# Cached attention with an MLP beside it, on one core: all large loads in one in-order stream through a ring of slots, a softmax per group of four key heads, scores in four column tiles, output weights last

## The chip, the cores and the metric

The kernel runs on one core of a Trainium2 chip. Times are device microseconds (us) of the whole program, medians of several executions. A profile's "span" runs from the first to the last instruction; in the runs that list both it is 1.7 to 2.0 us shorter than the time of its own run. PE is the matmul engine (PEld its weight loads, which overlap it), DVE the vector engine, ACT the scalar engine, POOL the general one, SP the one that issues DMAs. SBUF and PSUM are the memories that tiles lie in; the matmuls here write to PSUM.

## The reference, cut to what matters

Eight sequences, one new token each, bf16. Of a cache of 4096 keys the last 1024 are used; 16 query heads share 8 key heads of 256 numbers.

```
q = (x @ wq)                                   # x [8, 448], wq [448, 16*256]
scores = q . k_cache[:, :, -1024:, :] / 16     # per sequence and head: 1024 scores
o = softmax(scores) @ v_cache[:, :, -1024:, :]
a = o @ wo                                     # wo [4096, 448]
b = gelu(layernorm(x) @ w1 + b1) @ w2 + b2     # w1 [448, 1792], w2 [1792, 448]
out = g * a + (1 - g) * b                      # g = sigmoid(sum(x * gate_w))
```

Keys and values are 67.1 MB, the four weight matrices 10.6 MB. Each byte is used once, so there are 77.7 MB to read and little arithmetic to each byte.

## The kernel before

Work goes by pair (sequence, key head): 64 pairs. The keys of a pair are loaded, turned by 16 PE transposes, copied from PSUM to SBUF, and multiplied with a 128-column weight matrix that is zero except in the two columns of the pair's query heads. So all 128 columns of the array stream 512 keys for two useful rows, and the results of 32 pairs add up into one score tile. Softmax runs twice, over 64 rows each. The values of the first 32 pairs are used while the second 32 are scored.

```python
kpool = ctx.enter_context(tc.tile_pool(name="kpool", bufs=6))     # 512 KB each
# ...
def k_load(pidx):
    eng = nc.sync if (pidx % 2 == 0) else nc.scalar                # two queues
    eng.dma_start(Kn[:], A_k_cache[b, g, kv_base:Sk, :].rearrange("(p c) d -> p c d", c=NC8))
# ...
def k_scores(pidx):
    for j in range(NJ):
        for hf in range(NHALF):
            nc.tensor.matmul(
                S_ps[:, hf * NMM : (hf + 1) * NMM],
                lhsT=QTm[:, b, g, j, :],                           # 128 columns, 2 of them not zero
                rhs=KT[:, j, hf * NMM : (hf + 1) * NMM],
                start=(first and j == 0), stop=(last and j == NJ - 1),
            )
# ... w1, w2 and wo are loaded early, through the POOL queue:
nc.gpsimd.dma_start(w2_sb[:], B_w2.rearrange("(c p) n -> p c n", p=P))
nc.gpsimd.dma_start(wo_sb[:], A_wo.rearrange("(k p) n -> p k n", p=P))
# ...
for k in range(NBLK + 1):                                          # NBLK = 2, PB = 32
    if k == NBLK:
        mlp()
    for i in range(PB):
        if k < NBLK:
            k_load(nxt); k_transpose(nxt); k_scores(pidx)
        if k >= 1:
            v_load(qidx); pv(qidx)
    if k < NBLK:
        softmax_block(k)
# then 32 matmuls with the output weights, two DVE operations, the store
```

Of the kernel before, what the change touches and what calls it, by code (L numbers as in the profile page):

```python
# [9 lines left out]
ALU = mybir.AluOpType  # L10
AXIS = mybir.AxisListType
BF16 = mybir.dt.bfloat16
F32 = mybir.dt.float32


@with_exitstack
def kernel(
# [18 lines left out]
    B, Sq, D = A_x.shape  # L36
# [7 lines left out]
    NB = B * Sq  # L44
    assert Sq == 1 and Dh % P == 0 and W % P == 0 and F % P == 0
    assert NB * Hq == P, "layout assumes B*Sq*Hq == 128 rows"
    assert D % 32 == 0
    NJ = Dh // P
    NC8 = W // P
    NMM = 512  # L50
    NHALF = W // NMM
    NF = F // P
    NW = HD // P
    d_chunks = []
    d0 = 0
    while d0 < D:
        d_chunks.append((d0, min(P, D - d0)))
        d0 += P
    NDC = len(d_chunks)
    n_full = D // P  # L60
    tail = D - n_full * P
    assert 0 < tail < P and n_full >= 2
    qscale = float(Dh) ** -0.5

    NPAIR = NB * Hkv
    RB = 64
    assert P % RB == 0 and RB % Hq == 0
    NBLK = P // RB
    BPB = RB // Hq
    PB = BPB * Hkv  # L70

    xf = A_x.rearrange("b s d -> (b s) d")
    out_f = out.rearrange("b s d -> (b s) d")

    consts = ctx.enter_context(tc.tile_pool(name="consts", bufs=1))

    ident = consts.tile([P, P], BF16)
    make_identity(nc, ident[:])

    x_sb = consts.tile([NB, D], BF16)  # L80
    nc.sync.dma_start(x_sb[:], xf)

    QTm = consts.tile([P, NB, Hkv, NJ, P], BF16)
    qflat = QTm[:].rearrange("p a b c d -> p (a b c d)")
    qhalf = (NB * Hkv * NJ * P) // 2
    nc.vector.memset(qflat[:, 0:qhalf].bitcast(F32), 0.0)  # L86
    nc.gpsimd.memset(qflat[:, qhalf : 2 * qhalf].bitcast(F32), 0.0)  # L87

    oT_sb = consts.tile([P, Hq, NJ, NB], BF16)

    g_sb = consts.tile([NB, 1], F32)
    omg_sb = consts.tile([NB, 1], F32)
    bvec = consts.tile([NB, D], F32)

    wo_sb = consts.tile([P, NW, D], BF16)
    w1_sb = consts.tile([P, NDC, F], BF16)
    w2_sb = consts.tile([P, NF, D], BF16)
    b2_sb = consts.tile([1, D], BF16)
    ones_row = consts.tile([1, NB], BF16)
    nc.vector.memset(ones_row[:], 1.0)  # L100
    yT_sb = consts.tile([P, NDC, NB], BF16)

    mx = consts.tile([P, 1], F32)
    nmx = consts.tile([P, 1], F32)
    rowsum = consts.tile([P, 1], F32)
    rsum = consts.tile([P, 1], F32)
    E_raw = consts.tile([P, W], F32)
    E_bf = consts.tile([P, W], BF16)
    t1 = consts.tile([NB, D], F32)
    res = consts.tile([NB, D], BF16)  # L110

    psum_s = ctx.enter_context(tc.tile_pool(name="psum_s", bufs=1, space=bass.MemoryType.PSUM))
    S_ps = psum_s.tile([P, W], F32)

    kpool = ctx.enter_context(tc.tile_pool(name="kpool", bufs=6))
    ktpool = ctx.enter_context(tc.tile_pool(name="ktpool", bufs=4))
    etpool = ctx.enter_context(tc.tile_pool(name="etpool", bufs=2))
    psum_holder = {}
    K_tiles = {}

    def k_load(pidx):
        b, g = divmod(pidx, Hkv)
        Kn = kpool.tile([P, NC8, Dh], BF16, tag="kn")
        eng = nc.sync if (pidx % 2 == 0) else nc.scalar
        eng.dma_start(
            Kn[:],
            A_k_cache[b, g, kv_base:Sk, :].rearrange("(p c) d -> p c d", c=NC8),
        )
        K_tiles[("n", pidx)] = Kn

    def k_transpose(pidx):
        Kn = K_tiles.pop(("n", pidx))
        KT = ktpool.tile([P, NJ, W], BF16, tag="kt")
        for j in range(NJ):
            KTp = psum_holder["kt"].tile([P, W], BF16, tag="ktp")
            for c in range(NC8):
                nc.tensor.transpose(  # L137
                    KTp[:, c * P : (c + 1) * P],
                    Kn[:, c, j * P : (j + 1) * P],
                    ident[:, :],  # L140
                )
            if j == 0 or (pidx % 2 == 1):
                nc.vector.tensor_copy(KT[:, j, :], KTp[:])  # L143
            else:
                nc.scalar.copy(KT[:, j, :], KTp[:])  # L145
        K_tiles[("t", pidx)] = KT

    def k_scores(pidx):
        b, g = divmod(pidx, Hkv)
        KT = K_tiles.pop(("t", pidx))  # L150
        first = (pidx % PB) == 0
        last = (pidx % PB) == PB - 1
        for j in range(NJ):
            for hf in range(NHALF):
                nc.tensor.matmul(  # L155
                    S_ps[:, hf * NMM : (hf + 1) * NMM],
                    lhsT=QTm[:, b, g, j, :],
                    rhs=KT[:, j, hf * NMM : (hf + 1) * NMM],
                    start=(first and j == 0),
                    stop=(last and j == NJ - 1),  # L160
                )

    ET_tiles = {}

    def softmax_block(k):
        r0 = k * RB
        rs = slice(r0, r0 + RB)
        nc.vector.reduce_max(mx[rs, :], S_ps[rs, :], axis=AXIS.X)  # L168
        nc.vector.tensor_scalar_mul(nmx[rs, :], mx[rs, :], -1.0)
        nc.scalar.activation(  # L170
            E_raw[rs, :],
            S_ps[rs, :],
            ACT.Exp,
            bias=nmx[rs, :],
            scale=1.0,
            accum_out=rowsum[rs, :],
        )
        nc.vector.reciprocal(rsum[rs, :], rowsum[rs, :])
        nc.vector.tensor_scalar_mul(E_bf[rs, :], E_raw[rs, :], rsum[rs, :])  # L179
        ET_ps = psum_holder["sm"].tile([P, NC8, RB], BF16, tag="etp")  # L180
        for c in range(NC8):
            nc.tensor.transpose(  # L182
                ET_ps[:, c, :],
                E_bf[rs, c * P : (c + 1) * P],
                ident[rs, rs],
            )
        ET = etpool.tile([P, NC8, RB], BF16, tag="et")
        nc.vector.tensor_copy(ET[:], ET_ps[:])
        ET_tiles[k] = ET

    V_tiles = {}

    def v_load(pidx):
        b, g = divmod(pidx, Hkv)
        V = vpool.tile([P, NC8, Dh], BF16, tag="v")
        eng = nc.sync if (pidx % 2 == 0) else nc.scalar
        eng.dma_start(
            V[:],
            A_v_cache[b, g, kv_base:Sk, :].rearrange("(p c) d -> p c d", c=NC8),
        )  # L200
        V_tiles[pidx] = V

    PO_tiles = {}

    def pv(pidx):
        b, g = divmod(pidx, Hkv)
        k = pidx // PB
        ET = ET_tiles[k]
        V = V_tiles.pop(pidx)
        if g == 0:  # L210
            PO_tiles[b] = psum_holder["sm"].tile([P, Hkv, NJ, rep], F32, tag="po", name="PO")
        PO = PO_tiles[b]
        rloc = (b - k * BPB) * Hq + g * rep
        for j in range(NJ):
            for c in range(NC8):
                nc.tensor.matmul(  # L216
                    PO[:, g, j, :],
                    lhsT=V[:, c, j * P : (j + 1) * P],
                    rhs=ET[:, c, rloc : rloc + rep],
                    start=(c == 0),  # L220
                    stop=(c == NC8 - 1),
                )
        if g == Hkv - 1:
            for j in range(NJ):
                nc.vector.tensor_copy(  # L225
                    oT_sb[:, :, j, b].rearrange("p (g i) -> p g i", i=rep),
                    PO[:, :, j, :],
                )
            del PO_tiles[b]

    DEPTH = 2
    NPRO = min(DEPTH, NPAIR)

    with (
        tc.tile_pool(name="setup", bufs=1) as sp,
        tc.tile_pool(name="setup_ps", bufs=1, space=bass.MemoryType.PSUM) as sps,
    ):
        wq_sb = sp.tile([P, NDC, HD], BF16)
        nsplit = max(1, n_full - 1)
        nc.sync.dma_start(  # L240
            wq_sb[:, 0:nsplit, :],
            A_wq[0 : nsplit * P, :].rearrange("(c p) n -> p c n", p=P),
        )
        nc.scalar.dma_start(
            wq_sb[:, nsplit:n_full, :],
            A_wq[nsplit * P : n_full * P, :].rearrange("(c p) n -> p c n", p=P),
        )
        nc.gpsimd.dma_start(wq_sb[0:tail, n_full, :], A_wq[n_full * P : D, :])

        gw_sb = sp.tile([P, NDC], BF16)  # L250
        nc.gpsimd.dma_start(
            gw_sb[:, 0:n_full],
            gate_w[0 : n_full * P].rearrange("(c p) -> p c", p=P),
        )
        nc.gpsimd.dma_start(
            gw_sb[0:tail, n_full : n_full + 1],
            gate_w[n_full * P : D].rearrange("(p o) -> p o", o=1),
        )
        for pidx in range(NPRO):
            k_load(pidx)  # L260
        nc.gpsimd.dma_start(
# [112 lines left out]
    for pidx in range(NPRO):  # L374
        k_transpose(pidx)
# [126 lines left out]
```

## Time and profile before

| | before |
|---|---|
| time, median | 231.94 us (230.07 to 232.15, 3 runs) |
| span of the profile | 229.8 us |
| bytes moved | 78.06 MB, mean 340 GB/s |
| last V matmuls to the end | 13.7 us |

From the profile's page, kernel before. In part 2 each digit or number is one of 40 slices of the span: busy share in tenths, granted PE clock in tenths, GB/s.

```profile
span 229.8 us, 5695 instructions
PE   0005699994977799999999999888899696334693
PEclk9999999998899999999999999999999875555569
GB/s 238 351 301 407 318 377 344 353 390 409 406 410 411 406 354 316 295 303 301 317 351 412 406 407 406 409 406 410 407 406 407 311 78 406 410 406 409 130 0 1
L155 PE MATMUL S_ps<-KT,QTm 128*128 128x512 bf16 x229 | 61.3, 386 | 1.3
```

(229 of the 256 score matmuls are in the trace.) Where nothing disturbs it the DMA moves 406 to 412 GB/s. The row falls below that at the start, from slice 14 to 20, at slices 31 and 32, and in the tail. The windows view of the same trace shows what the engines do there (columns: stretch and length, busy us and instructions of each engine, granted clock, DMA share, GB/s).

```profile
50.00:80.00 30.00, 22.88 (x227) 14.86 (x228) 11.47 (x18) 6.07 (x6) 0.00 (x0) 0.94 1.02 408
80.00:120.00 40.00, 39.33 (x515) 29.56 (x523) 23.10 (x37) 11.43 (x13) 0.00 (x0) 1.00 0.93 319
180.00:188.00 8.00, 6.53 (x84) 3.44 (x84) 2.83 (x8) 0.71 (x3) 0.00 (x0) 0.79 0.32 128
```

From 80 to 120 us PE is busy 39.3 of 40 us, and key buffers come free too late: the stream waits for PE (the SP queue waits 29.4 us of it for the key transposes, by the waits view). From 180 to 188 us the second softmax and the MLP stand between the stream and the next free value buffer. The tail, from the timeline view (start, length, engine, line, operation, count, and in brackets the idle time before and what ended it):

```profile
216.12 0.58 PE L216 MATMUL PO<-ET,V 128*128 128x2 bf16 x16 [0.41 <-DMA V<-in_A_v_cache_dram]
217.02 8.91 PE L454 MATMUL A_ps<-wo_sb,oT_sb 128*8 128x448 bf16 x32 [0.32 <-DVE oT_sb L225]
225.98 0.67 DVE L462 TENSOR_SCALAR t_85<-A_ps,g_sb 8x448 f32<-8x448 f32 x1 [8.93 <-PE A_ps L454]
227.38 0.31 SPq L471 DMA_DIRECT2D out_dram<-res  x1
```

### The profile page before, as it was taken

The numbers are of one execution on the slowest core, as the hardware profiler recorded it, in microseconds if no ns is written. First come the engines' busy times: TensorE is split into PE (matmuls) and PEld (weight loads), VectorE is DVE, ScalarE is ACT, GpSimd is POOL, SyncE is SP. The second block draws the span as 40 slices with busy tenths as digits, with TensorE's granted clock in tenths as the row PEclk, the third lists the DMA queues.
The fourth block names the chain that finished last, engine by engine and source line by source line (L and its number), as shares of the span: only waits on it lengthen the run. The fifth ranks groups of instructions, "written<-read, shape, count | busy, mean of one in ns | idle before, by whom it ended". The sixth has DMA issues, their size and how long they took to land.

```text
span 229.8 us, 5695 instructions
## 1 busy us (share of the span) xinstructions
PE 174.4 (76%) x2536; PEld 129.7 (56%) x2563; DVE 81.0 (35%) x151; ACT 38.1 (17%) x41; POOL 11.3 (5%) x16
## 2 busy tenths in 40 slices
PE   0005699994977799999999999888899696334693
PEld 0005588573554477777778777667677375334431
DVE  6101303542334446559444444443443610000002
ACT  2001120111113131333132111112220200000000
POOL 9730000000000000000000000000000000000000
PEclk9999999998899999999999999999999875555569
DMA  6999999999999999899999999999999729999300
GB/s 238 351 301 407 318 377 344 353 390 409 406 410 411 406 354 316 295 303 301 317 351 412 406 407 406 409 406 410 407 406 407 311 78 406 410 406 409 130 0 1
DMA packets 20601, 78.06 MB, mean 340 GB/s; under 512 B 2304, under 2 KB 2352, under 8 KB 20128
## 3 DMA queue, kind: packets, MB, share of 16 engines
q1 hardware_dynamic: 9520, 35.67, 40.9%
q10 hardware_dynamic: 9360, 34.61, 39.6%
q0 software_dynamic: 1696, 7.41, 9.3%
q8 instruction: 20, 0.33, 0.6%
q14 instruction: 5, 0.04, 0.0%
HBM read 77.67 MB, written 0.01 MB: 338 GB/s over the span
## 4 chain that ended last, share of the span: by engine, by line
PE 53%; DMA 36%; DVE 4%; ACT 3%; issue 2%; SPq 1%; ACTq 0%; DVEq 0%
DMA Kn<-in_A_k_cache_dram 24%; PE KTp L137 18%; PE S_ps L155 18%; DMA V<-in_A_v_cache_dram 12%; PE PO L216 6%; PE qt L337 4%; PE A_ps L454 4%; ACT KT L145 3%; PE bb_ps L412 2%; DVE KT L143 2%; PE hT_ps L385 1%; DVE QTm L366 1%; PE ET_ps L182 0%; DVE E_bf L179 0%; DVE t_85 L462 0%
## 5 line engine op out<-in xcount | busy, mean ns | idle before, releaser
L143 DVE COPY KT<-KTp 128x1024 bf16<-128x1024 bf16 x96 | 63.6, 689 | 87.3 <-PE KTp L137 63.5
L137 PE MATMUL KTp<-ident,Kn 128*128 128x128 bf16 x1024 | 72.5, 226 | 27.6 <-DMA Kn<-in_A_k_cache_dram 23.5
L137 PEld LDWEIGHTS <-Kn 128*128 128x128 bf16 x1024 | 63.3, 101 | 38.5 <-DMA Kn<-in_A_k_cache_dram 28.7
L155 PE MATMUL S_ps<-KT,QTm 128*128 128x512 bf16 x229 | 61.3, 386 | 1.3
L145 ACT COPY KT<-KTp 128x1024 bf16<-128x1024 bf16 x32 | 32.4, 1012 | 128.3 <-PE KTp L137 74.2
L216 PEld LDWEIGHTS <-V 128*128 128x128 bf16 x1024 | 32.0, 99 | 23.0 <-DMA V<-in_A_v_cache_dram 13.9
L216 PE MATMUL PO<-ET,V 128*128 128x2 bf16 x1024 | 32.9, 164 | 14.6 <-DMA V<-in_A_v_cache_dram 13.1
L155 PEld LDWEIGHTS <-QTm 128*128 128x128 bf16 x256 | 22.7, 99 | 16.6 <-issue 1.8
L225 DVE CAST oT_sb<-PO 128x16 bf16<-128x16 f32 x16 | 2.5, 221 | 29.9 <-PE PO L216 29.8
L337 PE MATMUL qt<-xT_sb,wq_sb 128*128 128x8 bf16 (+1 forms) x128 | 10.0, 178 | 0.0
L337 PEld LDWEIGHTS <-wq_sb 128*128 128x128 bf16 (+1 forms) x128 | 8.6, 108 | 1.3 <-issue 0.2
L454 PE MATMUL A_ps<-wo_sb,oT_sb 128*8 128x448 bf16 x32 | 8.9, 456 | 0.3 <-DVE oT_sb L225 0.3
L454 PEld LDWEIGHTS <-oT_sb 128*8 128x8 bf16 x32 | 3.4, 106 | 5.5 <-issue 3.5
L366 DVE TENSOR_SCALAR QTm<-qt 128x128 bf16<-128x128 f32 x2 | 1.2, 798 | 10.4 <-PE qt L337 10.4
L412 PE MATMUL bb_ps<-w_sb,hT_sb 128*8 128x448 bf16 x14 | 4.3, 479 | 0.0
L86 DVE MEMSET QTm<- 128x4096 f32 x1 | 3.5, 3472 | 1.7 <-PEq L486 1.7
L280 PE MATMUL misc<-ident,x_sb 8*128 8x8 bf16 (+1 forms) x4 | 0.4, 175 | 4.8 <-POOL ident masks.py:199 4.8
L462 DVE TENSOR_SCALAR t_85<-A_ps,g_sb 8x448 f32<-8x448 f32 x1 | 0.7, 672 | 8.9 <-PE A_ps L454 8.9
L87 POOL MEMSET QTm<- 128x4096 f32 x1 | 3.5, 3516 | 0.0
L168 DVE TENSOR_REDUCE mx<-S_ps 64x1 f32<-64x1024 f32 x2 | 2.4, 1222 | 2.6 <-PE S_ps L155 2.5
L170 ACT ACTIVATE E_raw<-S_ps,nmx 64x1024 f32<-64x1024 f32 x2 | 2.2, 1108 | 6.4 <-DMA V<-in_A_v_cache_dram 6.4
L280 PEld LDWEIGHTS <-x_sb 8*128 8x128 bf16 (+1 forms) x4 | 0.3, 106 | 4.7 <-issue 2.5
(55 smaller groups left out, 27.8 us busy)
## 6 DMA issues: line engine op xcount, KB each, us to landing
Kn<-in_A_k_cache_dram SPq DMA_DIRECT2D x32, 512.0 KB, 10.2
Kn<-in_A_k_cache_dram ACTq DMA_DIRECT2D x32, 512.0 KB, 9.6
V<-in_A_v_cache_dram SPq DMA_DIRECT2D x32, 512.0 KB, 10.2
V<-in_A_v_cache_dram ACTq DMA_DIRECT2D x32, 512.0 KB, 10.2
wo_sb<-in_A_wo_dram POOLq DMA_DIRECT2D x1, 3584.0 KB, 38.2
wq_sb<-in_A_wq_dram SPq DMA_DIRECT2D x1, 2048.0 KB, 14.5
w_sb<-in_B_w_dram POOLq DMA_DIRECT2D x1, 1568.0 KB, 28.7
w_sb<-in_B_w_dram POOLq DMA_DIRECT2D x1, 1344.0 KB, 17.4
```

Of the source, the lines that this page charges most:

```text
L86: nc.vector.memset(qflat[:, 0:qhalf].bitcast(F32), 0.0)
L87: nc.gpsimd.memset(qflat[:, qhalf : 2 * qhalf].bitcast(F32), 0.0)
L137: nc.tensor.transpose(KTp[:, c * P : (c + 1) * P], Kn[:, c, j * P : (j + 1) * P], ident[:, :],)
L143: nc.vector.tensor_copy(KT[:, j, :], KTp[:])
L145: nc.scalar.copy(KT[:, j, :], KTp[:])
L155: nc.tensor.matmul(S_ps[:, hf * NMM : (hf + 1) * NMM], lhsT=QTm[:, b, g, j, :], rhs=KT[:, j, hf * NMM : (hf + 1) * NMM], start=(first and ...
L216: nc.tensor.matmul(PO[:, g, j, :], lhsT=V[:, c, j * P : (j + 1) * P], rhs=ET[:, c, rloc : rloc + rep], start=(c == 0), stop=(c == NC8 - 1),)
L225: nc.vector.tensor_copy(oT_sb[:, :, j, b].rearrange("p (g i) -> p g i", i=rep), PO[:, :, j, :],)
L337: nc.tensor.matmul(qt[:, k, :], lhsT=wq_sb[:cw, ci, col0 : col0 + P], rhs=xT_sb[:cw, ci, :], start=(ci == 0), stop=(ci == NDC - 1),)
L366: nc.vector.tensor_scalar_mul(dest, src, qscale)
L412: nc.tensor.matmul(bb_ps[:, :], lhsT=hT_sb[:, f, :], rhs=w2_sb[:, f, :], start=(f == 0), stop=False,)
L454: nc.tensor.matmul(A_ps[:, :], lhsT=oT_sb[:, h, j, :], rhs=wo_sb[:, k, :], start=(k == 0), stop=(k == NW - 1),)
```

## The change

The intent: let one queue read everything, in the order in which it is used, as far ahead as the memory holds; make compute fit into the time of the stream group by group; leave little work behind the last load. The core of the diff, new side only, cuts marked:

```diff
+    RING = 19                                   # slots of 1 MB
+    def pump():                                 # issue loads while slots are free, in plan order
+        while len(slots) < min(len(plan), consumed[0] + RING):
+            t = ring.tile([P, SLOT], BF16, tag="slot", name="slot")
+            plan[len(slots)](t)                 # nc.sync.dma_start, always the SP queue
+            slots.append(t)
+    # the order of the stream
+    add_kv("k", A_k_cache, 0)
+    for r in range(NR):
+        add(("wq", r), rows_loader([wq_m[:, r, :]]))
+    add(("wq", NR), rows_loader([wq_t]))
+    for u in range(1, NQ):                      # NQ = 16 groups of 4 key heads
+        add_kv("k", A_k_cache, u)
+        add_kv("v", A_v_cache, u - 1)
+    add_kv("v", A_v_cache, NQ - 1)
+    add(("w1", 0), ...)  # w1 in 2 slots, w2 in 2 slots
+    for i in range(4):
+        add(("wo", i), rows_loader([wo_v[:, 4 * i : 4 * i + 4, :]]))
 ...
+    def scores(u):
+        for hf in range(W // NMM):
+            for j in range(NJ):
+                for a in range(QUAD):           # four heads, four column tiles
+                    nc.tensor.matmul(
+                        S_ps[32 * a : 32 * a + rep, hf * NMM : (hf + 1) * NMM],
+                        lhsT=qw[:, j, b, h0 : h0 + rep],
+                        rhs=KT[a][:, j, hf * NMM : (hf + 1) * NMM],
+                        start=(j == 0), stop=(j == NJ - 1),
+                    )
 ...
+    def mlp_hidden():
+        for c in range(NF):                     # NF = 14
+            for r in range(NR):                 # 3 matmuls of 128 columns, 14 elements apart
+                nc.tensor.matmul(hT[:, c, :], lhsT=w[:, o + c : o + F : NF], ...)
+            for h in range(2):                  # 2 matmuls of 64 columns, two column tiles
+                nc.tensor.matmul(hT[64 * h : 64 * h + 64, c, :],
+                                 lhsT=w1b[:, F + c : F + FH : NF], ...)
 ...
+    transpose_keys(0); norm_and_gate(); query(); scores(0); softmax(0)
+    for u in range(1, NQ):
+        transpose_keys(u)
+        values(u - 1, *weights(u - 1))
+        scores(u)
+        softmax(u)
+    hs = mlp_hidden()
+    values(NQ - 1, *weights(NQ - 1))
+    mlp_out(hs)
+    # 32 matmuls with wo, one DVE operation, the store
```

The eight PSUM copies of turned keys of a group go five to DVE and three to ACT. Program order is fixed by hand. The weights are loaded in rows of 1.8 to 8 KB, where the old kernel had 0.9 KB rows for w2 and wo.

## The prediction

> **What bounds the kernel now.** The DMA stream, with gaps. The page counts 78.06 MB; in undisturbed stretches of the windows view (50-80, 120-180 us) it moves 408 GB/s, so the bytes alone are 191 us of a 229.8 us span. The rest: 2 us before the first bytes; slow stretches (2-20 us at 345 GB/s, 20-50 at 358; 80-120 at 319, where PE is 98% busy and holds the key buffers; 180-188 at 128, where softmax and MLP hold the V slots), by the same arithmetic 3, 4, 9 and 5.5 us; and a tail without loads: the last V matmuls start at 216.1 us, 32 A_ps matmuls take 8.9 us, two DVE operations 1.35, the store 2.4: 13.7 us.
>
> **What the change does.** (a) One queue of 1 MB loads, 19 slots deep (48 us of stream). The Trainium skill ("DMA: Bandwidth & Descriptors", SWDGE vs HWDGE) lists one SP stream of 1 MiB loads with 4 KiB rows at 408.7 GB/s; this trace's 408 on two queues agrees. 77.7 MB at 408 is 190.3 us. (b) Score matmuls: now 256 of 512 columns at 0.215 us (4 in 0.86 us in the chain), 55 us. After, four column tiles side by side: by the skill ("TensorEngine Tiling (Array Packing)", Theoretical Speedup) up to 4x; nothing here shows it. I take 1.0-1.5 us per group of four heads, not 3.4. (c) A softmax runs 16 times, not 2: reduce 1.22 us, exp 1.3 us each, in front of the key copies. (d) Output weights last: the tail is short if PE has caught up.
>
> **Critical path.** A group moves 4.19 MB: 10.3 us of DMA. Its compute cycle, in program order with one score buffer: reduce 1.2, then eight key copies (5 on DVE at 0.69 us, 3 on ACT at 1.01 us behind the exp) gate 64 transposes through three PSUM buffers, about 5.5 us; softmax weights 1.5; 64 value matmuls at 25-30 ns, 1.8; scores 1.0-1.5: 9.8-10.8 us, an estimate from these durations. So compute nearly balances the stream, and the ring hides jitter. Half a microsecond over 10.3 would build 8 us of lag, about 5 us of it absorbed while w1, w2, wo load.
>
> **Tail.** w1 lands about 13 us before the last load. Then hidden layer (3-6 us, with tile switches), its DVE chain 2.2, last values 2.5, 14 mlp_out and 32 A_ps matmuls at 0.37 us cold, 0.19 warm, 10-12 us. PE ends 7-10 us after the last load, then DVE 0.7 and the store 2.4.
>
> **Sum.** 2 + 190.3 + 0.7 to landing = 193; + 8.5 + 3.1 = 205 span; + 1 us of compute lag; measured times lie 0.3-2.3 us above the span: **207 us**, range **200 to 218**. Chances: faster by over 2% 0.94, within 2% 0.04, slower 0.02.
>
> **What would show the steps right.** GB/s near 405-410 in every slice from 1 to 193 us; short waits of SP on slots; all reads done by 195 us; 4 score matmuls in 0.25-0.35 us; group period 10.3 us with PE waiting for DMA on K or V; 10-13 us from the last wo load to the end, A_ps in the chain.
>
> **What would make it wrong.** Column tiles not running together (3.4 us of scores per group): the cycle is over 12 us, the ring fills, GB/s falls to about 345, the time is 225-235 us. PE at half clock (transposes 0.9 us per tile): the same, weaker. Strided value weights slower than 25-30 ns. A queue below 408 GB/s: each 10 GB/s is 4.8 us. The tail fully warm: 200 us.

## The result and the profile after

212.7 us median (212.45 to 213.15, 4 runs) against 232.05 us (230.07 to 232.23, 4 runs) in the same rounds; the ratio is 0.918, interval 0.913 to 0.923. Ratios here are the mean time of one kernel's fast runs over that of the other's of the same rounds, so not quite the ratio of the medians.

From the page of the kernel after:

```profile
span 211.1 us, 6014 instructions
PE   0838989898888989679897988888859887195984
PEclk9995888887979796966979787888875797555599
GB/s 203 401 421 409 411 406 406 409 407 409 408 407 407 410 406 410 407 408 409 408 410 404 406 409 408 410 407 406 409 406 410 407 406 415 408 386 292 33 0 1
q1 hardware_dynamic: 20848, 77.68, 92.5%
q8 instruction: 21, 0.34, 0.7%
L300 PE MATMUL S_ps<-kt,qw 128*2 128x512 bf16 x256 | 24.9, 529 | 0.4 <-DVE qw L286 0.4
```

The GB/s row is flat from slice 1 to slice 34. All of the gain is there: the last packets of the last load end at 197.05 us, where before the last load ended at about 216.1 us (19.0 us later), while what follows the last load is 14.0 us long (before: 13.7). One queue is enough; 77.68 MB went through it.

One group of four heads, from the timeline (kernel after; lines of weight loads, DMA issues and some others left out):

```profile
30.45 1.87 PE L300 MATMUL S_ps<-kt,qw 128*2 128x512 bf16 x16
32.26 3.20 PE L259 MATMUL ktp<-ident,slot 128*128 128x128 bf16 x40
32.38 1.23 DVE L312 TENSOR_REDUCE nmx<-S_ps 128x1 f32<-128x1024 f32 x1 [1.55 <-PE S_ps L300]
33.64 1.11 ACT L315 ACTIVATE E<-S_ps,nmx 128x1024 bf16<-128x1024 f32 x1 [5.41 <-DVE nmx L312]
...
35.80 1.52 PE L259 MATMUL ktp<-ident,slot 128*128 128x128 bf16 x24 [0.34 <-ACT kt L263]
...
38.12 0.39 PE L335 MATMUL sm<-selr,ones_f 128*128 128x8 f32 x2 [0.62 <-DVE selr L325]
...
38.83 1.76 PE L352 MATMUL po<-ET,slot 128*128 128x2 bf16 x64 [0.31 <-DVE ET L337]
40.52 1.02 PE L300 MATMUL S_ps<-kt,qw 128*2 128x512 bf16 x8
```

From scores to scores it is 10.07 us (30.45 to 40.52), just under the 10.3 us in which the stream brings a group's 4.19 MB at 408 GB/s. (From 103 to 154 us, where scores take 1.03 us, the groups still follow each other every 10.0 to 10.4 us, and PE waits for keys.) Sixteen score matmuls take 1.87 us here; at full clock, at 103.46 us of the same trace, 1.03 us. One after the other, 16 at the 0.215 us of the old kernel would be 3.4 us. So the tiles do run together, 3.3 times as fast at full clock; the Trainium skill gives up to 4 times under "TensorEngine Tiling (Array Packing)", Theoretical Speedup.

The tail of the kernel after, from the timeline:

```profile
182.65 0.29 PE L374 MATMUL hT<-yT,slot 128*128 128x8 bf16 x2 [3.72 <-DMA slot<-in_B_w_dram]
184.37 0.28 PE L383 MATMUL hT<-yT,slot 128*64 128x8 bf16 x2 [0.33 <-DMA slot<-in_B_w_dram]
...
193.44 0.60 PE L335 MATMUL sm<-selr,ones_f 128*128 128x8 f32 x2 [2.17 <-DVE selr L325]
194.35 1.84 PE L352 MATMUL po<-ET,slot 128*128 128x2 bf16 x64 [0.31 <-DVE ET L337]
196.13 4.99 PE L419 MATMUL bb<-slot,hs 128*8 128x448 bf16 x14
201.89 6.21 PE L455 MATMUL A_ps<-slot,oT 128*8 128x448 bf16 x32 [0.76 <-DVE mixb L427]
208.14 0.67 DVE L462 SCALAR_TENSOR_TENSOR res<-A_ps,g_sb,mixb 8x448 bf16<-8x448 f32 x1 [6.30 <-PE A_ps L455]
208.84 0.32 SPq L470 DMA_DIRECT2D out_dram<-res  x1
```

Read it from the top: PE has been empty for 3.7 us when the first piece of w1 lands at 182.65 us, so compute is not late here. From 184.37 us, when the last piece has landed, one chain runs to the end: hidden layer to 190.9, its DVE operations and the row sums to 194.35, values 1.8, mlp_out 5.0, one DVE operation, A_ps 6.2, one DVE operation, the store. The loads of wo (the last of them in at 197.05) are long there when A_ps starts at 201.89. The clock row of the page has 5 in slices 34 to 37: PE runs at half speed. The Trainium skill describes under "TensorE: Matmul & The Clock Gate" (The HAM clock gate) that an idle PE is given half the clock and a busy one the full clock again. This trace agrees only in part. It has 0.50 from 176.7 to 200.6 us, through the wait for w1, and matmuls of 448 columns at 0.37 us there; but the clock fell before that wait, and from 184.4 to 190.9 us PE is busy without a gap, with the 8-column matmuls of the hidden layer, and the clock does not rise. What counts as busy is not shown here.

One more thing is odd. The loads of w1 ought to be in near 180 us (the bytes before its end at 408 GB/s), not at 184.4, and the stream does not stop sharply. The windows view of the kernel after:

```profile
192.00:193.00 1.00, 0.00 (x0) 0.00 (x0) 0.60 (x4) 0.30 (x1) 0.00 (x0) 0.50 0.81 296
193.00:194.00 1.00, 0.56 (x2) 0.53 (x3) 0.35 (x3) 0.00 (x0) 0.00 (x0) 0.50 0.60 229
194.00:195.00 1.00, 0.69 (x26) 0.64 (x25) 0.30 (x2) 0.00 (x0) 0.00 (x0) 0.50 0.55 208
195.00:196.00 1.00, 1.00 (x43) 1.00 (x41) 0.00 (x0) 0.00 (x0) 0.00 (x0) 0.50 0.33 125
196.00:197.00 1.00, 1.00 (x11) 0.46 (x9) 0.26 (x2) 0.00 (x0) 0.00 (x0) 0.50 0.29 101
```

The DMA share (last but one column) goes down in steps: some of the 16 engines have finished by 193 us, half are still at work at 194.5; from 195 to 197 us it is about a third. A load is complete only when its slowest engine is. The trace's completion records show how this comes about. A 1 MB load leaves 16 of them, one per engine:

```
completion records of one load, first to last (us)    spread
 13.4 -  13.8                                          0.4
 32.5 -  34.4                                          1.9
 73.3 -  75.2                                          1.9
 93.7 -  97.2                                          3.5
134.5 - 138.0                                          3.5
154.9 - 160.0                                          5.1
175.3 - 180.4                                          5.1
DMA packets of kind "instruction" (16 KB, 1.03 to 1.12 us each): 21 in the span;
the 1st at 20.19 us, the 9th at 83.94, the 17th at 154.57
```

The spread grows in three steps, each at a time at which a round of eight instruction packets begins. This is a coincidence in time until an experiment moves it (e6 and e8 do, and e11 at the end of the stream).

### The profile page after: what moved, and what is told of

Same layout as the page of the kernel before. It is cut to its first block, busy times and chain, and to the rows that moved or that the text cites. A ratio compares the mean times of both kernels' runs of the same rounds, so it can differ in the third digit from the quotient of the medians.

```text
span 211.1 us, 6014 instructions
## 1 busy us (share of the span) xinstructions
PE 167.2 (79%) x2718; PEld 134.2 (64%) x2718; DVE 93.8 (44%) x222; ACT 70.9 (34%) x86; POOL 0.8 (0%) x7
## 3 DMA queue, kind: packets, MB, share of 16 engines
q1 hardware_dynamic: 20848, 77.68, 92.5%
## 4 chain that ended last, share of the span: by engine, by line
DMA 46%; PE 33%; DVE 11%; ACT 6%; issue 2%; SPq 1%; ACTq 0%
DMA slot<-in_A_k_cache_dram 29%; DMA slot<-in_A_v_cache_dram 9%; PE ktp L259 9%; DMA slot<-in_B_w_dram 8%; PE po L352 6%; PE S_ps L300 6%; DVE kt L265 4%; PE A_ps L455 3%; DVE nmx L312 3%; ACT kt L263 3%; PE bb L419 2%; ACT E L315 2%; PE hT L374 2%; PE qt L276 2%; PE hT L383 1%
## 5 line engine op out<-in xcount | busy, mean ns | idle before, releaser
L259 PEld LDWEIGHTS <-slot 128*128 128x128 bf16 x1024 | 77.1, 117 | 28.5 <-DMA slot<-in_A_k_cache_dram 18.6
L259 PE MATMUL ktp<-ident,slot 128*128 128x128 bf16 x1024 | 83.1, 253 | 14.4 <-DMA slot<-in_A_k_cache_dram 9.3
L265 DVE COPY kt<-ktp 128x1024 bf16<-128x1024 bf16 x80 | 53.0, 688 | 28.5 <-PE ktp L259 27.5
L263 ACT COPY kt<-ktp 128x1024 bf16<-128x1024 bf16 x48 | 47.8, 1012 | 28.1 <-PE ktp L259 28.1
L315 ACT ACTIVATE E<-S_ps,nmx 128x1024 bf16<-128x1024 f32 x16 | 17.8, 1113 | 80.0 <-DVE nmx L312 80.0
L352 PEld LDWEIGHTS <-slot 128*128 128x128 bf16 x1024 | 30.0, 99 | 7.1 <-issue 6.2
L352 PE MATMUL po<-ET,slot 128*128 128x2 bf16 x1024 | 28.6, 164 | 5.7 <-DVE ET L337 5.0
L312 DVE TENSOR_REDUCE nmx<-S_ps 128x1 f32<-128x1024 f32 x16 | 19.6, 1225 | 20.0 <-PE S_ps L300 20.0
L300 PE MATMUL S_ps<-kt,qw 128*2 128x512 bf16 x256 | 24.9, 529 | 0.4 <-DVE qw L286 0.4
L335 PE MATMUL sm<-selr,ones_f 128*128 128x8 f32 x32 | 6.4, 272 | 8.7 <-DVE selr L325 8.7
L374 PEld LDWEIGHTS <-slot 128*128 128x128 bf16 x42 | 3.7, 151 | 5.8 <-DMA slot<-in_B_w_dram 5.6
L455 PE MATMUL A_ps<-slot,oT 128*8 128x448 bf16 x32 | 6.2, 352 | 0.8 <-DVE mixb L427 0.8
L393 DVE TENSOR_TENSOR z<-hT,b_sb 128x112 f32<-128x112 f32 x1 | 0.3, 274 | 10.8 <-PE hT L383 10.8
```

The source lines that it names most:

```text
L259: nc.tensor.transpose(ktp[:, c * P : (c + 1) * P], kn[:, o : o + P], ident[:])
L263: nc.scalar.copy(kt[:, j, :], ktp[:])
L265: nc.vector.tensor_copy(kt[:, j, :], ktp[:])
L300: nc.tensor.matmul(S_ps[32 * a : 32 * a + rep, hf * NMM : (hf + 1) * NMM], lhsT=qw[:, j, b, h0 : h0 + rep], rhs=KT[a][:, j, hf * NMM : (hf ...
L312: nc.vector.reduce_max(nmx[:], S_ps[:], axis=AXIS.X, negate=True)
L315: nc.scalar.activation(E[:], S_ps[:], ACT.Exp, bias=nmx[:], scale=1.0, accum_out=rowsum[:])
```

## The experiments

Eleven kernels ran after the prediction, all on the base of the kernel after. In all but e10 the result is correct. Medians in us; the ratio is to the kernel before of the same rounds.

| run | what | median | ratio |
|---|---|---|---|
| (after) | | 212.70 | 0.918 |
| e1_values_first | last values before the hidden layer | 209.08 | 0.899 |
| e2_hidden_grouped | hidden layer sorted by tile shape | 209.50 | 0.901 |
| e3_scores_untiled | scores through the whole array | 250.59 | 1.076 |
| e4_ring8 | 8 slots | 212.72 | 0.914 |
| e5_mlp_early | MLP behind the query weights | 204.55 | 0.879 |
| e6_values_moving | values moving, fewer PE instructions | 211.84 | 0.911 |
| e7_best | e2 + e5 + e6 | 204.43 | 0.879 |
| e8_moving_padded | e6 with its PE instructions filled up | 213.30 | 0.917 |
| e9_best_warm | e7 with fillers | 203.82 | 0.878 |
| e10_hidden_contiguous | e2, adjacent weights, wrong result | 207.93 (1 run) | |
| e11_fewer_rows | e9 with the query product turned round | 202.66 | 0.872 |

The kernel after was timed beside e1 to e11 only through the kernel before, which moved between 231.85 and 232.8 us; differences under 1 us between runs sent on different occasions are not to be read.

### Column tiles: e3

```diff
-                        S_ps[32 * a : 32 * a + rep, hf * NMM : (hf + 1) * NMM],
-                        lhsT=qw[:, j, b, h0 : h0 + rep],
+                        S_ps[:, hf * NMM : (hf + 1) * NMM],
+                        lhsT=qz[:, o : o + P],          # 128 columns, zero outside the head's two
-                        start=(j == 0), stop=(j == NJ - 1),
+                        start=(j == 0 and a == 0), stop=(j == NJ - 1 and a == QUAD - 1),
-    RING = 19
+    RING = 15
```

> The score matmuls use the whole array again (128-column weights, zero outside the head's two columns, all four heads accumulate into the same scores), one after the other; the ring has 15 slots to make room. In the changed kernel 16 score matmuls take about 1.85 us per group and the compute cycle of a group is 10.1 us against 10.3 us of DMA. Theory of the prediction (column tiles run together, and compute nearly balances the stream): scores 3.5 to 5 us per group, cycle 11.7 to 13 us, the stream falls to about 345 GB/s, total 232 to 250 us. Rival (PE has room, the gain comes from the order of the loads alone): under 218 us.

Measured: 250.6 us, slower than the kernel before. From the page and the timeline of e3:

```profile
GB/s 226 426 416 408 408 411 408 407 405 409 408 410 408 407 411 408 408 409 407 410 407 409 394 386 367 307 407 255 367 291 250 268 320 130 0 3 0 3 0 1
101.03 5.08 PE L308 MATMUL S_ps<-kt,qz 128*128 128x512 bf16 x15
```

A group's scores now take about 5 us, partly at half clock, and its cycle is 13.2 us (from one score phase at 101.03 to the next at 114.27). The 15 slots feed the stream for 22 slices, about 137 us, before it has to wait; then it runs at the pace of PE. So the load order alone does not give the gain: without the tiles the whole of it, and more, is lost. (The new order also has 16 softmax chains in front of the copies, where the old one had two; what they cost was not measured apart.)

### Depth of the ring: e4

```diff
-    RING = 19
+    RING = 8
```

> The ring has 8 slots instead of 19 (8 MB, 20 us of stream). Theory: since compute keeps pace with the stream group by group, a group holds at most 4 to 6 slots at once and the depth of 19 buys little: within 2 us of the changed kernel, 212 to 215 us. Rival (the depth hides waits between compute and stream): DMA gaps in every group, 218 us or more.

212.72 us: no loss. With compute at 10.07 us a group and DMA at 10.3, 8 slots are enough; the other 11 only let the stream run ahead. They do so at the end: with 8 slots the loads of wo wait for the hidden layer to free slots (8.3 us, by the waits view), and the last of them ends at 197.67 us instead of 197.05. The tail of this kernel hides that; one that ends soon after the last load need not.

### The tail: e1, e2, e10, e5

e1:

```diff
-    hs = mlp_hidden()
     values(NQ - 1, *weights(NQ - 1))
+    hs = mlp_hidden()
     mlp_out(hs)
```

> The last group's value matmuls (and the softmax weights they need) are put before the hidden layer of the MLP instead of after it; nothing else changes. In the changed kernel PE is empty from about 179 to 182.7 us (waiting for the w1 load), and after the hidden layer it waits 2.2 us for DVE and then spends 1.8 us on these matmuls before mlp_out. Theory (the tail behind the landing of w1 is one serial chain on PE, DVE and ACT): 2.5 to 3.5 us faster than the changed kernel, about 209.7 us; the stream ends at the same time; mlp_out starts near 193 us instead of 196.1. Rival (the end is set by the last load of the output weights, landing near 195 us): no change, 212.7 us.

209.08 us, 3.6 us less than the kernel after, as the theory said; the rival falls. mlp_out starts at 193.10 us instead of 196.13:

```profile
193.10 4.16 PE L419 MATMUL bb<-slot,hs 128*8 128x448 bf16 x14 [2.13 <-DVE hs L412]
```

e2:

```diff
-                    start=(r == 0),
+                    start=(c == 0 and r == 0),
 ...
+        for c in range(NF):                     # a loop of its own for the 64-column matmuls
             for h in range(2):
```

> The hidden layer's 42 full-width matmuls run first and its 28 matmuls of 64 columns after them, instead of alternating 3 and 2. Same matmuls, same data. In the changed kernel one round of 3 and 2 takes 0.485 us, 14 rounds 6.5 us. Theory (most of it is the switch between tile shapes, two per round): hidden layer 2.5 to 3.5 us, total about 209.5 us. Rival (the strided weight loads, 14 elements apart, are slow by themselves): hidden layer stays near 6 us, total 212 to 213 us. A middle value would mean both.

209.50 us. The hidden layer in e2:

```profile
183.43 2.56 PE L374 MATMUL hT<-yT,slot 128*128 128x8 bf16 x40 [0.86 <-DMA slot<-in_B_w_dram]
185.92 1.83 PE L384 MATMUL hT<-yT,slot 128*64 128x8 bf16 x28
```

68 matmuls in 4.25 us (183.43 to 187.68) where the alternating order needed 6.5 us from 184.37 on; those 2.3 us are the shape switches, some 85 ns each for 27 of them (an estimate), and nearly 1 us more is that the 64-column matmuls no longer make the others wait for the last piece of w1. That a change of tiling mode drains PE is what the Trainium skill says under "TensorEngine Tiling (Array Packing)", Key Properties. The time fell as the theory said, but the layer itself did not come down to 2.5 to 3.5 us. The 40 full-width matmuls take 62 ns each (2.49 us), where the value matmuls, also at half clock, take 29 ns. e10 asks why:

```diff
-                    lhsT=w[:, o + c : o + F : NF],
+                    lhsT=w[:, o + c * P : o + (c + 1) * P],      # wrong hidden units on purpose
```

> As e2_hidden_grouped, but the 42 full-width matmuls of the hidden layer take 128 adjacent columns of w1 as weights instead of columns 14 apart. The hidden units come in the wrong order, so the result is wrong on purpose; times and bytes are comparable. In e2_hidden_grouped these matmuls take 62 ns each at half clock. Theory (weights that are 28 bytes apart load slowly): about 27 to 32 ns each, as the value matmuls at the same clock. Rival (half clock is the reason): 62 ns again.

```profile
183.43 1.23 PE L374 MATMUL hT<-yT,slot 128*128 128x8 bf16 x40 [0.93 <-DMA slot<-in_B_w_dram]
```

29 ns each (1.15 us for 40): the stride of 28 bytes doubled the time of a weight load. The Trainium skill has 16-byte lines in SBUF ("SBUF — State Buffer", the Door 1 section, its note on cachelines), so that a stride of up to 8 bf16 numbers costs nothing; the stride of 2 in the value weights (29 ns) and of 14 here (62 ns) agree. No run tries a stride between them. (e10's result is wrong by 3%, and its 207.93 us are a single run.)

e5:

```diff
     add(("wq", NR), rows_loader([wq_t]))
+    add(("w1", 0), ...) ... add(("w2", 1), ...)   # moved up from behind the last values
 ...
     scores(0)
     softmax(0)
+    mlp_out(mlp_hidden())
 ...
-    hs = mlp_hidden()
     values(NQ - 1, *weights(NQ - 1))
-    mlp_out(hs)
```

> The four MLP weight loads stand in the stream behind the query weights instead of behind the last values, and the whole MLP is computed before the second group. Bytes and matmuls are the same. Theory (the 16 us between the last landing near 195 us and the end are the serial MLP chain, and only 8 A_ps matmuls, one DVE operation and the store need to follow the last load): 3 us of matmuls at half clock, 0.7, 2.4: span 201 to 202, time about 203 us. Rival (the MLP work moved into the first 35 us makes compute late, and as a group's compute of 10.1 us hardly gains on the 10.3 us of DMA, it stays late to the end): a lag of 4 to 5 us remains, 206 to 209 us.

204.55 us, 8 us less than the kernel after. There is no lag left at the end (PE waits for keys again at 177.7 us), so the rival falls. The 1.5 us that the theory misses: A_ps ran at half clock until 196.2 us and took 8.55 us in one piece, and I had misread when the last load lands (next part).

```profile
191.46 8.55 PE L454 MATMUL A_ps<-slot,oT 128*8 128x448 bf16 x32
```

### Instruction fetches and the last load: e6, e8, e7, e9, e11

e6 turns the value product round, which halves its 2048 PE instructions:

```diff
-                    for c in range(NC):                 # 64 a group, V is the weights
-                        nc.tensor.matmul(PO[:, j, rep * a : rep * (a + 1)],
-                            lhsT=vn[:, o + j : o + Dh : NJ], rhs=ET[:, c, rep * a : rep * (a + 1)], ...)
+        for c in range(NC):                             # 32 a group, V moves
+            for a in range(QUAD):
+                nc.tensor.matmul(PO_ps[32 * a : 32 * a + rep, :],
+                    lhsT=ET[:, c, rep * a : rep * (a + 1)], rhs=vn[a // 2][:, o : o + Dh], ...)
+        # scaled by 1 / row sum on DVE, then two small matmuls turn it
```

> The value product with the softmax weights stationary (2 columns) and V moving (256 columns), in four column tiles, 32 matmuls a group for 64; the result is scaled by the reciprocal row sums and turned by two small matmuls; the separate matmul that spreads the row sums falls away. PE's program shrinks from 5390 to 4414 rows. In the changed kernel the 16 completion records of one 1 MB load spread over 0.4 us before 20 us, 2.0 from 22 us, 3.5 from 84 us and 5.0 us from 155 us, each step at the time of the 1st, 9th and 17th record of kind instruction (16 KB each, 1.07 us). Theory (instruction fetches occupy 8 of the 16 DMA engines in turn and make these late; PE's program is what is fetched): 17 records instead of 21, the third step comes late or not at all, the last load's spread is 3.5 us for most of the end, w1 lands 1 to 1.5 us earlier; with the shorter tail (values 0.9 us less, row sums 0.6 less) 209 to 211 us; the group's compute falls to 8.5 to 9.3 us and PE waits for DMA instead. Rival (the spread grows with the bytes moved, whatever is fetched): spread again 5.0 us from 155 us on.

e8 has e6's code and data with idle repetitions:

```diff
-        for c in range(NC):
+        for c in list(range(NC)) * 5:
             nc.tensor.matmul(sm[:, c, :], lhsT=E[:, c * P : (c + 1) * P], rhs=sel[:], start=True, stop=True)
```

> As e6_values_moving, but each of the 8 small matmuls that turn the softmax weights is issued five times, so that PE's program has 5438 rows again; data, loads and results are the same. Theory of the instruction fetches: 21 or 22 records of kind instruction, spread of the last loads 5.0 us again, third step near 155 us, 0.5 to 2 us slower than e6. Rival (spread from the bytes moved): no difference in spread between e6 and e8.

The queue's line on the page, the windows view at the end, and from the timeline the matmuls that wait for the last piece of w1; e6 first, then e8:

```profile
q8 instruction: 17, 0.28, 0.5%
195.00:196.00 1.00, 0.95 (x5) 0.45 (x6) 0.23 (x1) 0.00 (x0) 0.00 (x0) 0.50 0.17 54
196.00:197.00 1.00, 1.00 (x4) 0.29 (x3) 0.00 (x0) 0.00 (x0) 0.00 (x0) 0.50 0.00 0
182.80 0.28 PE L389 MATMUL hT<-yT,slot 128*64 128x8 bf16 x2 [0.36 <-DMA slot<-in_B_w_dram]
```

```profile
q8 instruction: 21, 0.34, 0.7%
195.00:196.00 1.00, 0.00 (x0) 0.00 (x0) 1.00 (x1) 0.00 (x0) 0.00 (x0) 0.50 0.39 140
196.00:197.00 1.00, 0.69 (x4) 0.35 (x5) 0.48 (x2) 0.00 (x0) 0.00 (x0) 0.50 0.18 68
184.05 0.28 PE L389 MATMUL hT<-yT,slot 128*64 128x8 bf16 x2 [0.34 <-DMA slot<-in_B_w_dram]
```

And from the completion and packet records:

```
                            after   e6      e8      e7      e9      e11
PE instructions in the code 5390    4414    5438    4414    4456    4278
instruction packets         21      17      21      17      17      16
17th of them at (us)        154.6   195.2   155.0   190.2   187.5   none
last wo packets end (us)    197.05  195.49  196.73  197.01  196.78  195.49
DMA engines busy at 195 us  8       8       9       8       8       8
engines loading at 196.5    4       0       4       1       1       0
```

With 17 packets, the last of them as the stream ends, the spread stays at 3.5 us from 114 us to the end; with the same data and code but 21 packets the third step is back, at 155 us. So the number of PE instructions makes the loads late, not the bytes moved: the packets come to floor(instructions / 256), and a round of eight of them delays eight of the 16 engines by 1.5 to 1.7 us each. At 195 us eight or nine engines are still at work, and at 196.5 us four still load in the kernel after and in e8, one in e7 and e9, none in e6 and e11: as many as there are packets from the 17th on that begin before 195 us. (The count of five in the expectation of e11 below takes in the 21st packet itself, at 196.03 us.) In e1, e5 and e10, where the 21st begins before 194 us, five engines end after 196.4 us.

In time, e8 is 1.5 us slower than e6, and the traces say where: the last piece of w1 is in 1.25 us later (184.05 against 182.80), and each step of the chain behind it is 1.26 us later, up to the start of mlp_out. The extra matmuls of e8 are done there while DVE still works on the hidden layer. The last 0.27 us arise in mlp_out (5.35 us against 5.08).

The 0.9 us between the kernel after and e6 were measured on two occasions and are too few to be read. e6 missed its time (211.84, not 209 to 211): w1 was in 1.6 us earlier, as expected, but at half clock the values of the tail were no shorter (1.88 us, before 1.84), and the scaling took 1.35 us on DVE.

e7 puts e2, e5 and e6 together:

> All together: MLP early, its hidden layer grouped by tile shape, values with V moving. Theory: the early MLP no longer leaves a lag, since the group's compute has over 1 us of room; end of the stream near 194 to 195 us, then 8 A_ps matmuls, one DVE operation, the store: span 199 to 201, time 201 to 202.5 us. If the tail behind the last load is longer than 7 us, the cause is still open.

204.43 us, no better than e5: the fetches again. The tail no longer outlasts the load by much, but its 17th packet comes at 190.2 us, and one engine, held up a third time, finishes the last load at 197.0 us. The last eight A_ps matmuls wait for it:

```profile
197.50 1.67 PE L463 MATMUL A_ps<-slot,oT 128*8 128x448 bf16 x8 [0.37 <-DMA slot<-in_A_wo_dram]
```

e9 adds matmuls that nobody reads, to keep the clock up:

```diff
+    filler(10)                       # 512 columns each, from the identity and an old key tile
     values(NQ - 1, *weights(NQ - 1))
+    filler(6)
     turn()
 ...
+        if h in (3, 11):
+            filler(2 if h == 3 else 3)
```

> As e7_best, with 21 matmuls of 512 columns whose result nobody reads, put where PE would wait at the end: ten before the last values, six before the last turn, two and three between the matmuls of the output weights. In e7_best the last load landed at 195.2 us, but A_ps ran at half clock (0.37 us a matmul from 189.6 us on) and ended at 199.2, the program at 202.2. Theory (the half clock of a PE that has waited is what is left of the tail): A_ps at 0.19 us a matmul, end of A_ps near 197 us, span 200, time 2 us less than e7_best: about 202.3 us. Rival (the fillers only take PE's time, or the clock does not rise from them): 204 us or more.

203.82 us. The clock is at 1.00 from 180 us on and A_ps runs at about 0.2 us a matmul, as the theory said, but of the expected 2 us no more than 0.6 came out, less than can be read between two occasions: the last load lands hardly earlier (196.8 us), PE, now fast, waits for the first three pieces of wo, and the last eight A_ps matmuls stand behind three fillers until 197.32 us. The theory had the right mechanism and the wrong limit.

e11 takes the 17th packet away:

```diff
-            for k in range(Hq * NJ):                    # 128 matmuls, wq is the weights
-                nc.tensor.matmul(qt[:, k, :], lhsT=w[:, c : c + P], rhs=xT[:, r + half, :], ...)
+            for n in range(8):                          # 32 matmuls, wq moves, four column tiles
+                a, bank = n % QUAD, n // QUAD
+                nc.tensor.matmul(S_ps[32 * a : 32 * a + NB, bank * 512 : bank * 512 + 512],
+                    lhsT=xT[:, r + half, :], rhs=w[:, c : c + 512], ...)
+        # one scaled copy, eight small matmuls that turn it, eight small copies
```

> As e9_best_warm with one filler less, and with the query product turned round (8 columns of x stationary, 512 columns of wq moving, in four column tiles, then eight small matmuls that turn the result), which cuts PE's program from 4456 to 4278 rows. A correction first: the last load did not land at 195.2 us, as the expectations before this one say (that was the one before it); its last packets end at 197.05 us in the changed kernel, 195.5 in e6_values_moving, 197.0 in e7_best and 196.8 in e9_best_warm, and at 195 us 8 of the 16 DMA engines are still busy, at 196.5 us 5, 0, 1 and 1 of them. The 17th instruction fetch comes at 190.2 us in e7_best and 187.5 in e9_best_warm, at 195.2 in e6. Theory: with under 17 times 256 rows there is no 17th fetch in the stream, the last packets end at 195.5 us, and the program ends 1.0 to 1.7 us earlier than e9_best_warm: span 200.3 to 201, time about 202.3 us. Rival (the last load's end has another cause): its packets end at 196.8 to 197 us again and the time is 203.8 us.

202.66 us (5 rounds), span 200.7 (e9: 202.0), and 195.49 us for the last packets, as the theory said. The 1.2 us to e9 are from two occasions, and the ratios' intervals overlap (0.868 to 0.876, 0.873 to 0.883); the time of the last packets is the clearer sign. The end in e11:

```profile
195.00:196.00 1.00, 0.93 (x5) 0.23 (x4) 0.00 (x0) 0.00 (x0) 0.00 (x0) 1.00 0.18 66
196.00:197.00 1.00, 1.00 (x6) 0.48 (x6) 0.00 (x0) 0.00 (x0) 0.00 (x0) 1.00 0.00 0
198.37 0.32 SPq L508 DMA_DIRECT2D out_dram<-res  x1
```

This is the best kernel: 0.872 of the kernel before, and 0.95 of the kernel after by the two ratios (0.8716 / 0.9179). In it, 5.2 us follow the last packet (195.5 to 200.7), most of it fillers and eight matmuls, one DVE operation and the store.

## Why the prediction was right or wrong

The time, 212.7 us, lies in the range of 200 to 218 and the direction is as forecast; the centre, 207, was 5.7 us too low.

- **"What bounds the kernel now: the DMA stream, with gaps."** Right: the gaps went, and they were the gain. The tail, which I had listed as a fifth loss, did not shrink (13.7 to 14.0 us).
- **One queue at 408 GB/s.** Right: 401 to 421 GB/s in slices 1 to 34, with one queue, as "DMA: Bandwidth & Descriptors" has it (408.7).
- **Column tiles at 1.0 to 1.5 us a group.** The mechanism is right (e3: 250.6 us without). The size is right at full clock (1.03 us) and low at half clock (1.87 us), which is what the first eight groups (to 95 us) and the last two had.
- **A compute cycle of 9.8 to 10.8 us against 10.3.** Right: 10.07, with scores at half clock. The allowance of 1 us for lag was not needed: PE waited for w1.
- **"193" for the last load.** Wrong by 4 us: 197.05. The term is the sum "2 + 190.3 + 0.7 to landing": it took all 16 DMA engines to finish together. The mean stream was as fast as predicted, but the fetches of PE's instructions hold up eight of the engines, four of them three times, and each load is as late as its slowest engine (e6, e8, e11). In e11, without a 17th packet, the last packets end at 195.49.
- **"w1 lands about 13 us before the last load", PE ends "7-10 us after the last load".** w1 was in at 184.37, 12.7 us before the last load, but PE ended at 208.1, 11.1 us after it. The mis-sized terms: the hidden layer took 6.5 us, not 3 to 6 (tile switches about 2.3 us in e2, strided weights about 1.3 us in e10), and between it and mlp_out passed 5.2 us, not 4.7; also A_ps waited 0.8 us for a DVE operation that I had not counted, since both use one PSUM buffer.
- **The sum.** 4.0 us (last load) and 2.6 us (11.1 for 8.5) more, 1.0 us of lag less, and the time 1.6 us above the span where some 1 us was allowed: less 0.5 us for rounding and a slightly shorter end, the 5.7 us.
- **Signs.** "All reads done by 195 us" and "10 to 13 us from the last load to the end" failed narrowly (197.05, 14.0), and both pointed at the true place. "4 score matmuls in 0.25-0.35 us" held at full clock (0.26) and not at half clock (0.47).

Not settled: on which engine each instruction packet ran is inferred from the steps and from the counts of busy engines; the packet records do not name the engine. Why a packet of 1.03 to 1.12 us makes its engine 1.5 to 1.7 us late is not shown, nor why in the kernel after four more engines end at 194.5 us that are done by 193.2 us in e6 and e11. No run keeps two queues, or the old sizes and rows of the loads, in the new order: what each of these did for the gapless stream is not separated.

## What to carry to other kernels

When a kernel is bound by its loads, first make the stream gapless, for which here one in-order queue with 8 slots was enough, and a compute cycle that fits under the loads group by group was needed (e4, e3); then look only at what follows the last byte, and move work that does not need that byte (here the whole MLP, 8 us) to the front. A load is as late as its slowest DMA engine, so read the decline of the DMA share at the end of the stream as well as the mean rate, and count instructions: the same product with the operands exchanged can need half as many. In a tail, ask of each matmul at which clock it runs, but a faster PE gains nothing where it then waits for the last load.

## What the Trainium skill lacked or had wrong

- "Runtime: NRT & Kernel Launch" (Instruction fetch mechanics) has instructions fetched in 16 KiB blocks of 256 and calls the cost of a block mostly hidden; no page, "DMA: Bandwidth & Descriptors" included, says what the fetches cost a stream of loads. Here the blocks were packets of 1.03 to 1.12 us, one per 256 of PE's instructions, and each round of eight made part of the engines 1.5 to 1.7 us later (spread of one load's completions 0.4, 1.9, 3.5, 5.1 us).
- "TensorE: Matmul & The Clock Gate" (Weight-path perf modes) lists the fast weight load's reads as "packed or strided"; 128 weights 28 bytes apart took 62 ns a matmul against 29 ns for adjacent ones (e2, e10). The line size in "SBUF — State Buffer" fits, but no page applies it to strided weight loads.
- "TensorEngine Tiling (Array Packing)" says that a change of tiling mode drains PE, without a figure: here about 85 ns a change at half clock (an estimate, 2.3 us for 27, e2).
- The same page gives "Up to 4×" for four column tiles as a theoretical speedup, without a measurement: here 16 matmuls of 512 columns took 1.03 us at full clock, against 3.4 us one after the other (an estimate, 16 at 0.215 us), 3.3 times.
